# Thirteen float64 weight pieces loaded into buffers of their own at the start of a fused attention and MoE kernel

## The chip, the cores and the metric

One core of a Trainium2 chip runs the whole program in one launch. The metric is the device time of that core in microseconds (us), lower is better. Engines are named as the profile names them: PE is TensorE (PEld its weight loads), DVE is VectorE, ACT is ScalarE, POOL is GpSimd, SP is SyncE. A letter q behind a name (SPq, ACTq) marks the engine's own instruction queue, from which it also issues DMAs.

## The reference, cut to what matters

Windowed attention with sink tokens over 4 batches, 8 heads, 768 positions and head size 64, then a dense two-layer block with a squared ReLU, then a top-1 mixture of eight experts. The weights of the dense block come in as float64.

```
keep   = is_sink | (0 <= rel < window)
a      = softmax(where(keep, q @ k.T / 8, -1e9))
x      = (a @ v)  as [3072, 512]
h      = maximum(x @ moe_w_in, 0)            # moe_w_in  [512, 2048], float64
x      = (h * h) @ moe_w_out                 # moe_w_out [2048, 512], float64
e      = argmax(x @ w_gate)
out    = softmax(x @ w_gate)[e] * sigmoid(x @ w_output_gate[:, e]) * (maximum(x @ w1[e], 0) @ w2[e])
```

## The kernel before

The 3072 tokens go through attention and the dense block in NBLK = 12 blocks of 256 tokens, t = 0 to 11; after that comes the expert part in slots of 128 tokens. Matrices of the dense block are kept as a high and a low half in the PE's fast 4-byte type (float32r in the code), and a product is three matmuls (high by high, high by low, low by high). For the first two blocks (t below T32 = 2) attention uses plain float32 matmuls.

The float64 weights are brought in as 32 pieces, c = 0 to 31, by `conv(c)` (lines 261 to 285). Piece c = 2j is the j-th strip of moe_w_in (`WI[:, j]`), piece c = 2j + 1 the j-th strip of moe_w_out (`WO`, in two tiles WOa and WOb of eight strips each). A piece is one DMA of 512 KB on SP (L265 or L269) into a tile `craw` of 4 KB a partition, tag "stage", three buffers that set-up tiles and others share. Then its `rest()` runs: two ACT operations on the raw words (L275, L276), two DVE operations that join them to a float32 in `fbuf` (L278, L279), one copy that makes the high half, on ACT if c is a multiple of 3 and else on DVE (L281 or L283), and one POOL subtraction that makes the low half (L284). `fbuf` holds two pieces.

`cstep(n)` (lines 750 to 758) emits the loads two pieces ahead and then the `rest()` of the next n pieces. Thirteen calls stand between the attention steps of the first block (line 791, every third value of h from -39), before `split_x(0)` on line 793. In block t = 0, line 932 emits pieces 13 to 16 ahead of j = 0 and then one piece a step. The first layer of block t and step j, `l1(t, j)` (L546), reads strip 2j; the second layer, `l2` (L562), reads piece 2j + 1 two steps later.

Attention of a block is a list of events (`attn_events`) run at half steps: `prep_k` and `prep_q` transpose the loaded keys and queries (L319, L345), `scores` (L400, or L404 from t = 2 on), masks, exponentials and scaling on DVE and ACT (L408 to L424), `ptrans` (L439, L443), `pv` (L472, or L479 from t = 2 on). Attention of block t + 1 runs beside the dense layers of block t. The loads of keys, queries and values come from `loads(t, p)` two head pairs ahead, each into two buffers (L306). `split_x(t)` (L512, L513) makes both halves of a finished block's `xT`, which has one buffer: it marks the border between two blocks.

The order of instructions on each engine is fixed when the program is built: a planner takes instructions by priority when its cost model says that their inputs are there. Priority is program order, but attention events ahead of h = 0 are moved up by 200 and the dense layers of block 0 by 20 (lines 777 and 933); pieces and `split_x` are not moved. [...]

Of the kernel before, what the change touches and what calls it, by code (L numbers as in the profile page):

```python
# [8 lines left out]
F32 = mybir.dt.float32  # L9
F32R = mybir.dt.float32r  # L10
# [24 lines left out]
LEADS = ((5, 2, 4.5, 8.5), (5, 2, 4.5, 8), (5.5, 2.5, 4.5, 8))  # L35

SPLITS = {6: (0, 0), 8: (2, 0), 11: (0, 1), 12: (1, 0), 13: (2, 1), 14: (3, 0)}
NSLOT = NT // 128 + NE - 1
PRE = 2

# [2 lines left out]
def kern(ctx, tc, q, k, v, n_sink, window, w_in, w_out, w_gate, w_og, w1, w2, out):  # L43
# [216 lines left out]

    def conv(c):
        j, which = divmod(c, 2)
        raw = cv.tile([128, 512, 2], I32, tag="stage", bufs=3, name="craw")
        if which == 0:
            SY.dma_start(out=raw[:].rearrange("p (k f) w -> p k (f w)", k=4),  # L265
                         in_=w_in.bitcast(I32)[:, 256 * j:256 * j + 256].rearrange("(k p) f -> p k f", p=128))
            hi, lo = (WI[:, j, n].rearrange("p k f -> p (k f)") for n in range(2))
        else:
            SY.dma_start(out=raw[:].rearrange("p f w -> p (f w)"), in_=w_out.bitcast(I32)[128 * j:128 * j + 128, :])  # L269
            hi, lo = (WO[j // 8][:, j % 8, n] for n in range(2))  # L270

        def rest():
            L, Hh = raw[:, :, 0], raw[:, :, 1]

            A.activation(out=Hh.bitcast(F32), in_=Hh.bitcast(F32), func=AF.Copy, scale=2.0 ** -112)  # L275
            A.activation(out=L, in_=L.bitcast(U32), func=AF.Copy, scale=0.93 * 2.0 ** -29)  # L276
            f, fi = fbuf[:, c % 2], fbuf[:, c % 2].bitcast(I32)
            V.scalar_tensor_tensor(out=fi, in0=Hh, scalar=3, in1=L, op0=ALU.logical_shift_left, op1=ALU.bitwise_or)  # L278
            V.scalar_tensor_tensor(out=fi, in0=Hh, scalar=-2147483648, in1=fi, op0=ALU.bitwise_and, op1=ALU.bitwise_or)  # L279
            if c % 3 == 0:  # L280
                A.activation(out=hi, in_=f, func=AF.Copy)  # L281
            else:
                V.tensor_copy(out=hi, in_=f)  # L283
            G.tensor_tensor(out=lo, in0=f, in1=hi.bitcast(F32), op=ALU.subtract)  # L284
        return rest
# [9 lines left out]
    def loads(t, p):  # L295
        b, u = divmod(t, NQ // 2)
        s0 = 256 * u
        for nm, src, m in (("k", k, 3), ("q", q, 2), ("v", v, 3)):
            x = att.tile([128, m, 2, D], F32, tag=nm + "n", name=nm + "n", bufs=2)
            lo = s0 - 128 * (m - 2)  # L300
            o = 0
            if lo < 0:
                lo, o = 0, 1
            nb = m - o
            for e in range(2):
                (A if nm == "q" and t == 0 and p < 2 else SY).dma_start(out=x[:, o:m, e, :],  # L306
                             in_=src[b, 2 * p + e, lo:lo + 128 * nb, :].rearrange("(n s) d -> s n d", s=128))
            nat[nm, t, p] = x
# [438 lines left out]
    rests = {}  # L747
    st_ = dict(load=0, done=0)

    def cstep(n):  # L750
        for _ in range(n):
            if st_["done"] >= NC:
                return
            while st_["load"] < min(NC, st_["done"] + 2):
                rests[st_["load"]] = conv(st_["load"])
                st_["load"] += 1
            rests.pop(st_["done"])()
            st_["done"] += 1

# [5 lines left out]
    with tc.If(gv > 0):  # L765
        with tc.tile_pool(name="genp", bufs=1) as gp_:
            general(gp_)
    wpool2 = ctx.enter_context(tc.tile_pool(name="wpool2", bufs=1))
    WO[1] = wpool2.tile([128, NF // 2, 2, 512], F32R, name="WOb")
    WOf[1] = WO[1][:].rearrange("p j a f -> p (j a f)")  # L770
    events = sorted((e for t in range(NBLK) for e in attn_events(t)), key=lambda e: e[0])
    events.reverse()

# [13 lines left out]
    for h in range(-46, 0):  # L787
# [2 lines left out]
            setup2()  # L790
        if h >= -39 and h % 3 == 0:
            cstep(1)
    split_x(0)

    raw = None
# [303 lines left out]
```

## Time and profile before

| | us |
|---|---|
| median of 3 runs | 1198.46 (1195.75 to 1199.82) |
| the profiled execution | 1196.3 |
| its span in the trace | 1194.5 |
| start to `split_x(0)` | about 59 |
| block t = 0, to `split_x(1)` | 59 to 155.4 |
| a later block | some 60 to 62 |

The span is what the trace covers; 1.8 us of the profiled execution lie around it. Busy times are sums over an engine's instructions within a stretch; a matmul's end is modelled, so a busy PE can still run below its full pace. A table by stretch shows first the length, then each engine's busy time with the number of instructions, then the granted clock of TensorE as a share of full speed, the DMA engines' busy share and their rate.

### The profile page before, as it was taken

The numbers are of one execution on the slowest core, as the hardware profiler recorded it, in microseconds if no ns is written. First come the engines' busy times: TensorE is split into PE (matmuls) and PEld (weight loads), VectorE is DVE, ScalarE is ACT, GpSimd is POOL, SyncE is SP. The second block draws the span as 40 slices with busy tenths as digits, with TensorE's granted clock in tenths as the row PEclk, the third lists the DMA queues.
The fourth block names the chain that finished last, engine by engine and source line by source line (L and its number), as shares of the span: only waits on it lengthen the run. The fifth ranks groups of instructions, "written<-read, shape, count | busy, mean of one in ns | idle before, by whom it ended". The sixth has DMA issues, their size and how long they took to land. (4 is left out here: it accounts for less than half of the span.)

```text
span 1194.5 us, 24037 instructions
## 1 busy us (share of the span) xinstructions
PE 1138.7 (95%) x7022; PEld 945.7 (79%) x7022; DVE 761.5 (64%) x2123; ACT 626.5 (52%) x1740; POOL 457.9 (38%) x949
## 2 busy tenths in 40 slices
PE   4898889999999999999999999999899999999996
PEld 2476678888888888888888888887788888888884
DVE  4699776767676667676767677656611466764153
ACT  3677576767666766666676666545222222222200
POOL 4256665326565335555424556310211222222111
PEclk9999899999999999999999999999999999999998
DMA  4565411111211211121112120087411357554110
GB/s 123 132 181 176 137 35 45 32 51 37 54 32 28 50 37 46 35 49 29 47 35 51 37 54 1 19 182 207 133 39 44 100 179 255 189 203 151 42 51 23
DMA packets 139387, 100.08 MB, mean 84 GB/s; under 512 B 103903, under 2 KB 112223, under 8 KB 139234
## 3 DMA queue, kind: packets, MB, share of 16 engines
q1 hardware_dynamic: 132674, 83.85, 25.1%
q0 software_dynamic: 5472, 14.19, 3.6%
q8 instruction: 64, 1.05, 0.4%
q14 instruction: 89, 0.73, 0.3%
q10 hardware_dynamic: 1088, 0.26, 0.1%
HBM read 85.56 MB, written 13.76 MB: 83 GB/s over the span
## 5 line engine op out<-in xcount | busy, mean ns | idle before, releaser
L546 PE MATMUL psh<-xT,WI 128*128 128x256 f32 x2304 | 314.8, 285 | 10.6 <-POOL WI L284 8.1
L546 PEld LDWEIGHTS psh<-xT,WI 128*128 128x128 f32 x2304 | 294.9, 190 | 29.0 <-POOL WI L284 10.9
L867 PE MATMUL psh<-WI,xt 128*128 (+1 forms) x672 | 164.8, 400 | 0.3 <-ACT ht L847 0.3
L562 PE MATMUL psx<-WOb,h 128*128 128x512 f32 x576 | 157.8, 410 | 2.7 <-ACT h L552 2.4
L562 PE MATMUL psx<-WOa,h 128*128 128x512 f32 x576 | 159.0, 409 | 0.0
L867 PEld LDWEIGHTS psh<-WI,xt 128*128 128x128 f32 x672 | 124.3, 188 | 27.9 <-ACT xt L847 0.5
L550 DVE TENSOR_TENSOR r<-r 128x256 f32<-128x256 f32 x184 | 83.6, 455 | 68.3 <-ACT r L549 66.7
L562 PEld LDWEIGHTS psx<-WOb,h 128*128 128x128 f32 x576 | 102.6, 191 | 23.4 <-ACT h L552 3.9
L412 ACT ACTIVATE P<-P,st 128x260 f32<-128x260 f32 (+1 forms) x192 | 92.7, 485 | 47.4 <-DVE st L410 45.1
L883 DVE TENSOR_TENSOR ht<-psht,ht 128x512 fp32r<-128x512 f32 x56 | 38.5, 689 | 123.9 <-ACT ht L847 123.5
L549 ACT ACTIVATE r<-psh 128x256 f32<-128x256 f32 x192 | 72.2, 377 | 83.6 <-PE psh L546 72.4
L562 PEld LDWEIGHTS psx<-WOa,h 128*128 128x128 f32 x576 | 102.1, 190 | 17.4 <-issue 0.3
L553 DVE TENSOR_TENSOR h<-r,h 128x256 fp32r<-128x256 f32 x192 | 91.9, 479 | 29.3 <-ACT h L552 25.7
L905 POOL DMA_INDIRECT out_dram<-xg,pidx x28 | 31.2, 1116 | 193.5 <-ACT xg L904 152.0
L408 DVE CUSTOM_DVE_ANT_0 P<-pss,M 128x260 f32<-128x260 f32 (+1 forms) x184 | 72.5, 403 | 28.2 <-PE pss L404 14.3
L455 POOL TENSOR_SCALAR_AFFINE_SELECT PT<-PT 128x256 fp32r<-128x256 f32 x224 | 85.1, 415 | 12.9 <-DVE st L410 12.8
L552 ACT ACTIVATE h<-r 128x256 fp32r<-128x256 f32 x192 | 78.1, 408 | 22.2 <-DVE r L550 18.0
L896 PE MATMUL psy<-WOb,ht 128*128 (+1 forms) x336 | 85.1, 402 | 0.0
L896 PE MATMUL psy<-WOa,ht 128*128 (+1 forms) x336 | 84.1, 397 | 0.0
L873 ACT ACTIVATE r<-psh 128x512 f32<-128x512 f32 x48 | 28.7, 598 | 99.7 <-PE psh L867 97.8
L838 POOL DMA_INDIRECT xg<-x2tab,pidx x30 | 40.7, 1356 | 95.5 <-issue 55.9
L489 POOL TENSOR_TENSOR xr<-tB,tC 128x128 f32<-128x128 f32 x80 | 37.6, 470 | 97.8 <-DVE tB L488 95.3
(430 smaller groups left out, 1979.3 us busy)
## 6 DMA issues: line engine op xcount, KB each, us to landing
raw<-in_moe_w_dram SPq DMA_DIRECT2D x36, 1024.0 KB, 6.2
craw<-in_moe_w_in_dram SPq DMA_DIRECT2D x16, 512.0 KB, 3.8
craw<-in_moe_w_out_dram SPq DMA_DIRECT2D x16, 512.0 KB, 3.2
x2tab<-x2s SPq DMA_DIRECT2D x24, 256.5 KB, 3.1
kn<-in_k_dram SPq DMA_DIRECT2D x64, 96.0 KB, 2.3
vn<-in_v_dram SPq DMA_DIRECT2D x64, 96.0 KB, 2.2
qn<-in_q_dram SPq DMA_DIRECT2D x92, 64.0 KB, 2.1
kn<-in_k_dram SPq DMA_DIRECT2D x32, 64.0 KB, 2.1
```

Of the source, the lines that this page charges most:

```text
L408: V.tensor_tensor_reduce(out=P[:, e, 0:W], in0=ps[e][:, 0:W], in1=mask[:, 0:W], scale=1.0, scalar=-3.0e38, op0=ALU.add, op1=ALU.max, accum ...
L412: A.activation(out=P[:, e, 0:W], in_=P[:, e, 0:W], func=AF.Exp, scale=SCALE, bias=st[:, 2 + e:3 + e], accum_out=st[:, 4 + e:5 + e])
L455: G.affine_select(out=both[:, 1 - b, e], in_=bf[:, 0, e], pattern=[[0, 2], [1 - 2 * b, 128]], compare_op=ALU.is_gt if b else ALU.is_ge, fi ...
L546: PE.matmul(ps[:], lhsT=WI[:, j, a_, kk, :], rhs=x[:, b_, kk, :], start=(n == 0), stop=(n == 11))
L549: A.activation(out=hq[:], in_=ps[:], func=AF.Relu)
L550: (G if t == 0 and j % 2 else V).tensor_tensor(out=hq[:], in0=hq[:], in1=hq[:], op=ALU.mult)
L552: A.activation(out=o[:, 0], in_=hq[:], func=AF.Copy)
L553: V.tensor_tensor(out=o[:, 1], in0=hq[:], in1=o[:, 0].bitcast(F32), op=ALU.subtract)
L562: PE.matmul(acc[t][m][:], lhsT=o[:, a_, 128 * m:128 * m + 128], rhs=WO[j // 8][:, j % 8, b_, :], start=(j == 0 and n == 0), stop=(j == NF ...
L838: G.indirect_dma_start(out=x, out_offset=None, in_=x2tab[:] if s >= PRE else x2tab[0:256 * (NBLK - 3)], in_offset=bass.IndirectOffsetOnAxi ...
L867: PE.matmul(ps[:], lhsT=o[:, a_, kk, :], rhs=wview(n, par + 2048 * b_ + 512 * kk, 512), start=(c == 0), stop=(c == 11))
L896: PE.matmul(yp[s][:], lhsT=o[:, a_, kk, :], rhs=wview(2 + n, par + 2048 * b_ + 512 * kk, 512), start=(n == 0 and kk == 0 and c == 0), stop ...
```

## The change

The first thirteen pieces get buffers of their own: six raw tiles `braw` and four float32 tiles in `bf`, in a pool "boot" that takes the place of WOb until the prologue is over (WOb is allocated after it is closed). The first six loads are issued at once on ACT's queue, right after the branch of the general case; loads 6 to 12 stay on SP, each into the raw tile of the piece six before it. From piece 13 on the stage tiles, `fbuf` and the distance of two pieces are as before. The high half is made on ACT unless c mod 3 is 1, so ten pieces (c = 2, 5, ... 29) go from DVE to ACT. The tiles of loaded values get a third buffer.

```diff
+NBOOT, BRAW = 13, 6
...
     def conv(c):
         j, which = divmod(c, 2)
-        raw = cv.tile([128, 512, 2], I32, tag="stage", bufs=3, name="craw")
+        if c < NBOOT:
+            raw = braw[c % BRAW]
+        else:
+            raw = cv.tile([128, 512, 2], I32, tag="stage", bufs=3, name="craw")
+        eng = A if c < BRAW else SY
         if which == 0:
-            SY.dma_start(out=raw[:].rearrange("p (k f) w -> p k (f w)", k=4),
+            eng.dma_start(out=raw[:].rearrange("p (k f) w -> p k (f w)", k=4),
...
-            f, fi = fbuf[:, c % 2], fbuf[:, c % 2].bitcast(I32)
+            f = bf[:, c % 4] if c < NBOOT else fbuf[:, c % 2]
+            fi = f.bitcast(I32)
...
-            if c % 3 == 0:
+            if c % 3 != 1:
                 A.activation(out=hi, in_=f, func=AF.Copy)
             else:
                 V.tensor_copy(out=hi, in_=f)
...
-            x = att.tile([128, m, 2, D], F32, tag=nm + "n", name=nm + "n", bufs=2)
+            x = att.tile([128, m, 2, D], F32, tag=nm + "n", name=nm + "n", bufs=3 if nm == "v" else 2)
...
+    def fetch():
+        while st_["load"] < max(min(NBOOT, st_["done"] + BRAW), min(NC, st_["done"] + 2)):
+            rests[st_["load"]] = conv(st_["load"])
+            st_["load"] += 1
+
     def cstep(n):
         for _ in range(n):
             if st_["done"] >= NC:
                 return
-            while st_["load"] < min(NC, st_["done"] + 2):
-                rests[st_["load"]] = conv(st_["load"])
-                st_["load"] += 1
+            fetch()
             rests.pop(st_["done"])()
             st_["done"] += 1
...
-    wpool2 = ctx.enter_context(tc.tile_pool(name="wpool2", bufs=1))
-    WO[1] = wpool2.tile([128, NF // 2, 2, 512], F32R, name="WOb")
-    WOf[1] = WO[1][:].rearrange("p j a f -> p (j a f)")
+    bootS = ExitStack()
+    boot = bootS.enter_context(tc.tile_pool(name="boot", bufs=1))
+    braw = [boot.tile([128, 512, 2], I32, name=f"braw{n}") for n in range(BRAW)]
+    bf = boot.tile([128, 4, 512], F32, name="bf")
+    fetch()
...
             cstep(1)
+    bootS.close()
+    wpool2 = ctx.enter_context(tc.tile_pool(name="wpool2", bufs=1))
+    WO[1] = wpool2.tile([128, NF // 2, 2, 512], F32R, name="WOb")
+    WOf[1] = WO[1][:].rearrange("p j a f -> p (j a f)")
     split_x(0)
```

## Rows read from the trace of the kernel before

**Rows 1.** The page's first part: busy time of an engine, its share of the span, and its instructions.

```profile
PE 1138.7 (95%) x7022; PEld 945.7 (79%) x7022; DVE 761.5 (64%) x2123; ACT 626.5 (52%) x1740; POOL 457.9 (38%) x949
```

**Rows 2.** Busy time by stretch: the prologue, block 0, block 1, and a later block. Columns: stretch, its length, busy time and instructions of PE, PEld, DVE, ACT and POOL, granted clock, DMA share, GB/s.

```profile
12.00:59.00 47.00, 37.94 (x138) 20.69 (x138) 28.14 (x106) 28.23 (x83) 13.59 (x35) 1.00 0.45 121
59.00:155.40 96.40, 84.05 (x442) 60.69 (x440) 88.51 (x178) 63.55 (x153) 61.47 (x77) 0.93 0.55 160
155.40:215.00 59.60, 58.94 (x428) 51.44 (x429) 42.17 (x151) 42.33 (x134) 32.69 (x85) 1.00 0.15 36
...
340.00:402.20 62.20, 60.76 (x441) 52.94 (x441) 43.98 (x156) 41.78 (x132) 32.39 (x83) 1.00 0.14 35
```

**Rows 3.** PE's waits in block 0 (59 to 155.4 us): who waited for whom, us in total, times, longest.

```profile
PE psh L546 <- POOL WI L284: 8.1, 8, 2.3
PE psh L546 <- DVE WI L283: 2.3, 3, 1.7
```

**Rows 4.** Busy time by stretch again, a stretch of 5 us within block 0; the granted clock stands third from the end.

```profile
135.00:140.00 5.00, 5.00 (x14) 3.22 (x14) 1.24 (x5) 1.51 (x4) 2.43 (x5) 0.50 0.47 149
```

**Rows 5.** Instructions in order of time near the end of block 0 (start, duration, engine, line): the low half of the last strip of moe_w_in on POOL, and the first-layer matmuls that read it.

```profile
149.92 1.71 POOL L284 TENSOR_TENSOR WI<-fbuf,WI 128x512 fp32r<-128x512 f32 x1
...
151.67 1.44 PE L546 MATMUL psh<-xT,WI 128*128 128x256 f32 x10 [1.22 <-POOL WI L284]
```

**Rows 6.** DVE's groups of instructions in block 0 (61.8 to 155.5 us): line, names, shapes, count, busy us, mean ns, idle before.

```profile
L278 DVE SCALAR_TENSOR_TENSOR fbuf<-craw 128x512 int32<-128x512 int32 x25 | 23.7, 948 | 4.2 <-ACT craw L276 3.4 <-POOL V L364 0.7 <-POOL psk L427 0.2
L279 DVE SCALAR_TENSOR_TENSOR fbuf<-craw,fbuf 128x512 int32<-128x512 int32 x25 | 20.4, 818 | 0.0
...
L414 DVE TENSOR_SCALAR st<-st 128x2 f32<-128x2 f32 x8 | 5.0, 621 | 0.0
...
L283 DVE CAST WOb<-fbuf 128x512 fp32r<-128x512 f32 x6 | 2.5, 417 | 0.0
```

**Rows 7.** DVE's groups in the prologue (12 to 59 us), same columns.

```profile
L279 DVE SCALAR_TENSOR_TENSOR fbuf<-craw,fbuf 128x512 int32<-128x512 int32 x6 | 4.1, 689 | 0.0
L278 DVE SCALAR_TENSOR_TENSOR fbuf<-craw 128x512 int32<-128x512 int32 x6 | 4.1, 684 | 3.9 <-ACT craw L276 3.9
...
L414 DVE TENSOR_SCALAR st<-st 128x2 f32<-128x2 f32 x10 | 1.6, 160 | 0.3 <-ACT P L412 0.3
```

**Rows 8.** PE's groups that differ between block 0 (61.8 to 155.5 us, the first two lines) and a later block (340 to 402.3 us, the last two lines), same columns.

```profile
L472 PE MATMUL pso<-PT,vn 128*64 128x128 f32 x56 | 9.5, 312 | 0.0
L439 PE MATMUL pspt<-ident,P 128*128 128x128 f32 x30 | 7.1, 306 | 0.1
...
L479 PE MATMUL pso<-PT,V 128*128 128x256 f32 x32 | 5.1, 281 | 0.0
...
L439 PE MATMUL pspt<-ident,P 128*128 128x128 f32 x16 | 3.5, 301 | 0.0
```

**Rows 9.** SP's DMA issues in order of time in the prologue: start, duration of the issue, line, what is loaded.

```profile
20.92 0.44 SPq L269 DMA_DIRECT2D craw<-in_moe_w_out_dram  x1
28.39 0.88 SPq L306 DMA_DIRECT2D vn<-in_v_dram  x2
...
32.47 0.42 SPq L265 DMA_DIRECT2D craw<-in_moe_w_in_dram  x1
...
43.09 0.40 SPq L269 DMA_DIRECT2D craw<-in_moe_w_out_dram  x1
```

**Rows 10.** Waits of SP's queue and of ACT in the prologue (12 to 62 us and 12 to 59 us): who waited for whom, us in total, times, longest.

```profile
SPq L306 <- PE psh L472: 19.7, 5, 7.1
...
ACT craw L275 <- SPq L765: 8.7, 1, 8.7
```

**Rows 11.** DMA issues of the whole span: what is loaded, queue, count, KB each, median us from issue to landing.

```profile
craw<-in_moe_w_in_dram SPq DMA_DIRECT2D x16, 512.0 KB, 3.8
```

**Rows 12.** PE in order of time in the prologue: the last product with the values (L472) of each of the four head pairs of block 0, by which a pair's attention ends.

```profile
27.24 1.12 PE L472 MATMUL psh<-PT,vn 128*64 128x128 f32 x4
...
35.13 1.13 PE L472 MATMUL psh<-PT,vn 128*64 128x128 f32 x8
...
44.45 1.13 PE L472 MATMUL psh<-PT,vn 128*64 128x128 f32 x8
...
56.03 0.69 PE L472 MATMUL psh<-PT,vn 128*64 128x128 f32 x2
```

**Rows 13.** DVE in order of time in the prologue: the first joining operation (L278) of five of the pieces.

```profile
18.03 0.68 DVE L278 SCALAR_TENSOR_TENSOR fbuf<-craw 128x512 int32<-128x512 int32 x1
...
35.64 0.68 DVE L278 SCALAR_TENSOR_TENSOR fbuf<-craw 128x512 int32<-128x512 int32 x1
...
41.51 0.69 DVE L278 SCALAR_TENSOR_TENSOR fbuf<-craw 128x512 int32<-128x512 int32 x1
...
45.66 0.68 DVE L278 SCALAR_TENSOR_TENSOR fbuf<-craw 128x512 int32<-128x512 int32 x1
...
53.11 0.69 DVE L278 SCALAR_TENSOR_TENSOR fbuf<-craw 128x512 int32<-128x512 int32 x1
```

**Rows 14.** The load of the keys of head pair 2 of block 0 on SP, and the first transpose of these keys on PE, in order of time.

```profile
14.40 0.89 SPq L306 DMA_DIRECT2D kn<-in_k_dram  x2
...
25.81 0.48 PE L319 MATMUL psk__758<-ident,kn 128*128 128x128 f32 x1
```

More of the change, by code (lines that the diff above doesn't have):

```diff
@@ L268, in conv @@
         else:
-            SY.dma_start(out=raw[:].rearrange("p f w -> p (f w)"), in_=w_out.bitcast(I32)[128 * j:128 * j + 128, :])
+            eng.dma_start(out=raw[:].rearrange("p f w -> p (f w)"), in_=w_out.bitcast(I32)[128 * j:128 * j + 128, :])
             hi, lo = (WO[j // 8][:, j % 8, n] for n in range(2))
```

## The prediction

> **What bounds the kernel now.** I read the page's busy shares first, then busy time by stretch, then the waits and groups inside the stretch that stands out. Over the whole span PE is busy 95% and DVE 64% [rows 1], which looks like a kernel bound by matmuls with nothing left on the vector side. The table by stretch says otherwise for its head [rows 2]. A later block takes 62.2 us with PE busy for 60.8 of them. Block 0 runs about the same number of matmuls (442 against 441 records) in 96.4 us; there DVE is busy for 88.5 us, twice the 44 us of a later block, while PE's granted clock averages 0.93. So block 0 runs at the pace of DVE, and what DVE has there that later blocks don't have is the conversion of the float64 pieces.
>
> The waits agree: in block 0 PE stands 8.1 + 2.3 = 10.4 us for the halves of moe_w_in [rows 3]. After such a stall the clock goes too: 0.50, the lower of its two levels, throughout 135 to 140 us [rows 4]. And the block's last strip is just in time: its low half is ready at 149.92 + 1.71 = 151.6 us, and the matmuls that read it start at 151.67 [rows 5]. When the last pieces are done sets when block 0 ends.
>
> The prologue is the other half of the picture: from 12 to 59 us DVE is busy for 28.1 us of 47, ACT for 28.2 [rows 2]. Only six of the pieces are joined there [rows 7], so 26 of 32 fall into the block where DVE has no room. Why so few? The loads came late. After 20.92 us SP issues no piece until 32.47, and the next after that at 43.09 [rows 9]: its queue stands at a load of values, whose buffer is free only after a product with the values (19.7 us in five waits, 7.1 the longest) [rows 10]. A piece takes 3.8 us to land [rows 11], so it is the order of the queue that holds the pieces back. DVE's joins show the hole: none starts between 18.03 and 35.64 us [rows 13].
>
> **The change, part by part.**
>
> *Loads.* Six loads leave SP's queue and go out on ACT's, ahead of everything that the values can block. Each issue takes about 0.44 us of the issuing engine [rows 9], 2.6 us in all. ACT stands idle for 8.7 us before its first piece operation [rows 10], so this is hidden; without that cover it would cost 2.6 us. SP's order gets six issues shorter, and the third buffer for values takes away most of the 19.7 us of waiting. What SP then waits for is a raw tile six pieces back; behind such a wait stand the loads of keys and queries. These have slack: the keys of pair 2 were issued at 14.40 and used at 25.81 us [rows 14]. Six loads at once are 3.1 MB. At the 512 KB in 3.8 us of a single load [rows 11] they would need 23 us in a row and end near 31 us; overlapping can only make it less. So all six are there before the time at which the third piece was joined (35.64) [rows 13]. No direct cost.
>
> [...]
>
> *Pieces that move.* With loads no longer late, thirteen pieces can be converted ahead of `split_x(0)` where six were: seven leave block 0. One piece costs DVE there 0.948 + 0.818 us for the joins and, for two in three, 0.417 us for the high half [rows 6], that is 2.04 us. Its subtraction on POOL also slows DVE: the 2-element L414 takes 0.621 us on average in block 0 and 0.160 in the prologue [rows 6, 7], 8 x 0.46 = 3.7 us over 26 pieces, 0.14 each. Seven pieces: 7 x 2.18 = 15.3 us of DVE time.
>
> [...]
>
> *High halves on ACT.* Ten pieces go from DVE to ACT; of pieces 13 to 31, six (14, 17, ... 29). DVE loses 6 x 0.417 = 2.5 us in block 0 [rows 6]. ACT is busy for 63.6 of 96.4 us there [rows 2] and takes them in its idle time.
>
> *Block 0, summed.* DVE's 88.5 us become 88.5 - 15.3 - 2.5 = 70.7. What is late next is PE. An estimate of its need: a later block's 62.2 us, plus the products with values, 9.5 against 5.1, and the transposes, 7.1 against 3.5 [rows 8], so 70.2 us. The two engines are now even. I keep the 7.9 us by which block 0 was longer than DVE's work (96.4 - 88.5): 78.6 us, a gain of 17.8. Ends: at best PE's need alone, 70.2, a gain of 26.2; at worst only three of the seven pieces move, 3 x 2.18 + 2.5 = 9.0.
>
> *The prologue pays.* Seven more pieces run between the steps of a chain in which attention of block 0 goes from engine to engine; an instruction of a piece that an engine has just begun holds up the next link. The trace shows what that does: the four pairs end at 28.4, 36.3, 45.6 and 56.7 us [rows 12], so pair 1 took 7.9 us with no join ahead of its end but the one at 35.64, pair 2 took 9.3 with the join at 41.51 and the rest of the piece begun at 35.64, pair 3 took 11.1 with those at 45.66 and 53.11 [rows 13]. Pair 2 gives (9.3 - 7.9)/2 = 0.7 us for a piece; pair 3 gives 1.6, but attention of block 1 has begun beside it. Below there is nothing to gain, since the pairs' inputs were early [rows 14]; the lower end is 0. I take 0.7, the cleaner of the two: 7 x 0.7 = 4.9 us, ends 0 and 11.2.
>
> *After block 0.* Blocks from 1 on are filled by PE (58.9 of 59.6 us in block 1) [rows 2], and nothing of the change touches them. A gain at 155 us goes through to the end.
>
> *Sum.* -17.8 + 4.9 = -12.9 us. Against the profiled execution's 1196.3 that is 1183.4; the median of the runs lies 2.2 us above that execution, so 1198.5 - 12.9 = **1185.6 us**. With the ends of the prologue's cost the forecast's own range is 1181 to 1192.
>
> **The rivals.**
>
> *1. PE alone is the bound.* If DVE really gets free, the clock stays at its upper level too and block 0 falls to 70.2 us. With half of the prologue's cost: -26.2 + 2.4 = -23.8, 1174.7 us. For it: the clock's dip stands behind a stall for a piece. Against it: DVE needs 70.7 us itself, and both engines work in a fixed order.
>
> *2. The pieces only change place.* The prologue grows by what block 0 loses on them, 15.3 us, because there too each piece stops the chain. Only the six high halves are left: -2.5, 1196.0 us. For it: pair 3's 1.6 us. Against it: 18.9 us of idle DVE from 12 to 59 us.
>
> *3. The change doesn't do what it says.* The pieces are loaded early but the fixed order still runs them after `split_x(0)`, or SP's waits for raw tiles hold back pieces 6 to 12. Again -2.5, 1196.0 us. Against it: pieces stand ahead of `split_x` in program order, and in the trace only late loads let it pass them.
>
> *4. Slower.* The place is DVE's queue from 12 to 59 us. If the chain meets each added piece in full, both joins (0.68 + 0.69) and then a subtraction as long as the 1.71 us of [rows 5], the prologue grows by 7 x 3.08 = 21.6 us against a gain of 17.8 in the block: +3.8, 1202.3 us, and with the block's low end 9.0, 1211. It decides from a prologue longer by 21.4 us, that is an end of pair 3 near 78 us.
>
> **How the numbers follow.** Chances: the forecast 0.59, rival 1 0.13, rival 2 0.12, rival 3 0.07, rival 4 0.09. 0.3% is 3.6 us, about what a measurement of this kernel can tell from no change. The forecast and rival 1 are faster by more: 0.72. Rivals 2 and 3 lie within: 0.19. Rival 4 is slower: 0.09. The range runs from rival 1 to past rivals 2 and 3, 1174 to 1199 us, leaving out rival 4 and what lies beyond rival 1's estimate.
>
> **What would show it.** Six issues of pieces on ACT's queue in a row near 8 us; joins of pieces between 18 and 36 us; twelve or thirteen joins ahead of `split_x(0)`, and that near 64 us (forecast), 59 to 61 (rival 1), 74 (rival 2) or past 78 (rival 4). Block 0 near 79 us, DVE busy for about 71 of them, PE's waits for halves of moe_w_in well under 10.4 us and the clock above 0.93. Blocks 1 to 11 unchanged. The prediction is wrong if fewer than ten pieces are joined before `split_x(0)`, or if block 0 stays above 88 us although they were.

## The result, and the profile after

The changed kernel is slower: 1212.53 us median (1209.52 to 1213.36) against 1197.11 (1192.90 to 1199.82) on the same chip, ratio 1.0127 with a 95% interval of 1.0103 to 1.0150. The forecast was 1185.6, faster. The profiled execution took 1213.36 us, its span 1211.4 against 1194.5.

Lines of the changed kernel are shifted: loads L272 and L276, scalings L282 and L283, joins L286 and L287, high half L289 (ACT) or L291 (DVE), low half L292, `split_x` L520 and L521, first layer L554, its relu L557, second layer L570. The page's first part answers to [rows 1]; the engines' totals have hardly moved, so the time lies in the order, not in the work:

```profile
PE 1139.9 (94%) x7022; PEld 947.5 (78%) x7022; DVE 764.0 (63%) x2113; ACT 631.8 (52%) x1750; POOL 462.2 (38%) x949
```

Busy time by stretch, columns as in [rows 2]: the prologue, the part of it after attention, block 0, five microseconds of block 0, block 1.

```profile
12.00:79.80 67.80, 43.25 (x154) 23.15 (x154) 41.62 (x124) 38.36 (x101) 22.12 (x43) 1.00 0.57 164
61.50:79.80 18.30, 0.00 (x0) 0.00 (x0) 18.30 (x23) 11.32 (x20) 12.08 (x8) 1.00 0.44 142
79.80:174.20 94.40, 81.43 (x433) 61.70 (x434) 78.55 (x154) 60.10 (x148) 54.96 (x75) 0.93 0.40 116
...
155.00:160.00 5.00, 5.00 (x17) 3.43 (x16) 2.20 (x7) 1.47 (x5) 0.00 (x0) 0.50 0.13 28
174.20:233.00 58.80, 58.43 (x424) 50.80 (x423) 41.30 (x151) 41.59 (x133) 30.37 (x78) 1.00 0.15 38
```

The borders say where the time is. `split_x(0)` moved from 59 to 79.8 us (+20.8), `split_x(1)` from 155.4 to 174.2 (+18.8), the span's end by +16.9. Block 0, in which 21 joins are left of 26, is shorter by 2.0 us only, and its clock dips as before [rows 4]. The loss is the stretch from 61.5 to 79.8 us, in which PE does nothing. PE's waits in block 0 and the stretch ahead of it (59 to 174 us; answers to [rows 3]): the waits for halves are gone, and two for `xT` have come.

```profile
PE psh L554 <- ACT xT L520: 18.8, 1, 18.8
PE psh L554 <- ACT r L557: 4.9, 6, 2.5
PE psh L554 <- DVE xT L521: 4.3, 1, 4.3
```

Why `xT` is late is read from ACT's instructions in order of time (ACTq are its DMA issues):

```profile
13.59 0.38 ACTq L272 DMA_DIRECT2D braw<-in_moe_w_in_dram  x1
13.99 0.53 ACTq L276 DMA_DIRECT2D braw<-in_moe_w_out_dram  x1
14.55 0.60 ACTq L272 DMA_DIRECT2D braw<-in_moe_w_in_dram  x1
...
21.14 0.35 ACTq L276 DMA_DIRECT2D braw<-in_moe_w_out_dram  x1
21.53 0.28 ACT L482 ACTIVATE xr<-psh 128x128 f32<-128x128 f32 x1 [3.00 <-DMA braw<-in_moe_w_in_dram]
...
28.81 0.37 ACTq L272 DMA_DIRECT2D braw<-in_moe_w_in_dram  x1
...
36.90 0.35 ACTq L276 DMA_DIRECT2D braw<-in_moe_w_out_dram  x1
...
42.50 0.67 ACT L282 ACTIVATE braw<-braw 128x512 f32<-128x512 f32 x1
...
56.88 0.67 ACT L282 ACTIVATE braw<-braw 128x512 f32<-128x512 f32 x1
...
79.83 1.32 ACT L520 ACTIVATE xT<-xr 128x256 fp32r<-128x256 f32 x4
```

The six loads don't leave in a row near 8 us. They stand in ACT's stream between attention's exponentials and copies, over 23 us. The fourth also holds ACT up: the 3.00 us of idle time in the row behind it end when an earlier load has landed, by 21.1 us. And the scalings are later than the loads: the first piece is scaled at 42.50, 28.9 us after its load was issued, with no idle time of ACT just before it, because the fixed order has it there. DVE's joins follow; the first three (answer to [rows 13], where the first is at 18.03 or earlier):

```profile
48.03 0.69 DVE L286 SCALAR_TENSOR_TENSOR bf<-braw 128x512 int32<-128x512 int32 x1
...
54.39 0.69 DVE L286 SCALAR_TENSOR_TENSOR bf<-braw 128x512 int32<-128x512 int32 x1
...
58.36 0.69 DVE L286 SCALAR_TENSOR_TENSOR bf<-braw 128x512 int32<-128x512 int32 x1
```

Two joins lie ahead of 56 us. Attention itself got faster: pair 3 ends at 53.9 us, 2.8 earlier than in [rows 12]. Then everything that had come late runs in one bulk, the conversion of nine pieces from 56.9 to 79.8 us on ACT, DVE and POOL, all of it ahead of `split_x(0)`, which has no priority and stands behind them in program order. PE in order of time:

```profile
53.22 0.69 PE L480 MATMUL psh<-PT,vn 128*64 128x128 f32 x2
...
80.28 0.80 PE L554 MATMUL psh<-xT,WI 128*128 128x256 f32 x2 [18.81 <-ACT xT L520]
...
85.40 4.85 PE L554 MATMUL psh<-xT,WI 128*128 128x256 f32 x21 [4.32 <-DVE xT L521]
```

### The profile page after: what moved, and what is told of

Its sections match the earlier page's. It is cut to its first block, busy times and chain, and to the rows that moved or that the text cites. A ratio compares the mean times of both kernels' runs of the same rounds, so it can differ in the third digit from the quotient of the medians.

```text
span 1211.4 us, 24030 instructions
## 1 busy us (share of the span) xinstructions
PE 1139.9 (94%) x7022; PEld 947.5 (78%) x7022; DVE 764.0 (63%) x2113; ACT 631.8 (52%) x1750; POOL 462.2 (38%) x949
## 5 line engine op out<-in xcount | busy, mean ns | idle before, releaser
L554 PE MATMUL psh<-xT,WI 128*128 128x256 f32 x2304 | 316.7, 286 | 28.0 <-ACT xT L520 18.8
L554 PEld LDWEIGHTS psh<-xT,WI 128*128 128x128 f32 x2304 | 296.8, 191 | 44.8 <-ACT xT L520 19.5
L570 PE MATMUL psx<-WOa,h 128*128 128x512 f32 x576 | 157.8, 408 | 1.5 <-DVE h L561 1.5
L570 PE MATMUL psx<-WOb,h 128*128 128x512 f32 x576 | 156.2, 409 | 0.8 <-ACT h L560 0.4
L570 PEld LDWEIGHTS psx<-WOb,h 128*128 128x128 f32 x576 | 102.9, 191 | 21.2 <-ACT h L560 1.5
L570 PEld LDWEIGHTS psx<-WOa,h 128*128 128x128 f32 x576 | 101.2, 189 | 19.3 <-DVE h L561 2.0
L557 ACT ACTIVATE r<-psh 128x256 f32<-128x256 f32 x192 | 72.3, 377 | 74.0 <-PE psh L554 63.4
L416 DVE CUSTOM_DVE_ANT_0 P<-pss,M 128x260 f32<-128x260 f32 (+1 forms) x184 | 72.7, 403 | 31.3 <-PE pss L412 17.0
L463 POOL TENSOR_SCALAR_AFFINE_SELECT PT<-PT 128x256 fp32r<-128x256 f32 x224 | 84.4, 412 | 12.6 <-DVE st L418 12.5
L913 PE MATMUL psy<-WOb,ht 128*128 (+1 forms) x336 | 85.1, 402 | 0.0
L855 POOL DMA_INDIRECT xg<-x2tab,pidx x30 | 45.6, 1519 | 95.8 <-issue 54.4
```

Of the source, the lines that this page charges most:

```text
L416: V.tensor_tensor_reduce(out=P[:, e, 0:W], in0=ps[e][:, 0:W], in1=mask[:, 0:W], scale=1.0, scalar=-3.0e38, op0=ALU.add, op1=ALU.max, accum ...
L463: G.affine_select(out=both[:, 1 - b, e], in_=bf[:, 0, e], pattern=[[0, 2], [1 - 2 * b, 128]], compare_op=ALU.is_gt if b else ALU.is_ge, fi ...
L554: PE.matmul(ps[:], lhsT=WI[:, j, a_, kk, :], rhs=x[:, b_, kk, :], start=(n == 0), stop=(n == 11))
L557: A.activation(out=hq[:], in_=ps[:], func=AF.Relu)
L570: PE.matmul(acc[t][m][:], lhsT=o[:, a_, 128 * m:128 * m + 128], rhs=WO[j // 8][:, j % 8, b_, :], start=(j == 0 and n == 0), stop=(j == NF ...
L855: G.indirect_dma_start(out=x, out_offset=None, in_=x2tab[:] if s >= PRE else x2tab[0:256 * (NBLK - 3)], in_offset=bass.IndirectOffsetOnAxi ...
```

## The experiments

My first theory was the late loads and the bulk. Its rivals were the bulk's place alone, the small parts of the change, and then the forecast's own frame: that block 0 runs at DVE's pace, so that pieces taken out of it are worth 2.2 us each. All medians stand against the kernel before on the same chip (1193.6 to 1194.9). "Start" is the first instruction of `split_x(0)`, "joined" the pieces whose first join came before it, "block 0" the time from there to `split_x(1)`, all of the profiled execution; "idle" is block 0 without PE's busy time, "clock" its granted clock. The executions of one kernel differ by up to some 11 us (e5: 1209.89 to 1220.67; before: 1192.90 to 1199.82), and the profiled ones of e5 and e9 were their fastest, 7.8 and 4.2 us below the median, so small differences between rows from "start" on say little. Kernels without a median leave weights out, so that later routing differs; each of them was run once.

| kernel | median | ratio | start | joined | block 0 | idle | clock |
|---|---|---|---|---|---|---|---|
| before | 1197.11 | 1 | 59.0 | 6 | 96.4 | 12.4 | 0.93 |
| after | 1212.53 | 1.0127 (1.0103-1.0150) | 79.8 | 11 | 94.4 | 13.0 | 0.93 |
| e1 loads on SP | 1199.83 | 1.0038 (1.0019-1.0057) | 59.5 | 5 | 99.8 | 14.9 | 0.91 |
| e2 split_x first | 1211.98 | 1.0147 (1.0116-1.0179) | 54.1 | 2 | 120.8 | 28.1 | 0.93 |
| e11 block first | 1217.12 | 1.0185 (1.0142-1.0228) | 54.0 | 2 | 120.4 | 29.1 | 0.89 |
| e5 loads first | 1217.71 | 1.0203 (1.0177-1.0229) | 72.7 | 12 | 98.6 | 14.9 | 0.86 |
| e6 spread | 1205.01 | 1.0084 (1.0060-1.0108) | 70.7 | 8 | 95.3 | 14.9 | 0.93 |
| e8 all early | 1209.15 | 1.0114 (1.0086-1.0141) | 81.0 | 16 | 89.7 | 5.0 | 0.92 |
| e3 high halves | 1201.22 | 1.0053 (1.0034-1.0072) | 51.8 | 5 | 104.9 | 18.2 | 0.89 |
| e4 third v | 1203.40 | 1.0069 (1.0043-1.0095) | 58.2 | 6 | 101.9 | 12.5 | 0.90 |
| e7 buffers only | 1206.36 | 1.0103 (1.0080-1.0125) | 56.0 | 6 | 110.3 | 21.9 | 0.89 |
| e9 more joins | 1209.79 | 1.0124 (1.0081-1.0168) | 56.8 | 6 | 103.8 | 17.4 | 0.89 |
| e10 fewer joins | | | 59.0 | 6 | 96.7 | 11.1 | 0.91 |
| e13 no piece in block 0 | | | 64.0 | 6 | 76.7 | 1.3 | 1.00 |
| e14 no pieces | | | 65.7 | 0 | 74.2 | 0.1 | 0.97 |
| e15 without 6 to 12 | | | 57.8 | 6 | 97.2 | 10.0 | 0.91 |
| e16 without last 7 | | | 60.6 | 6 | 86.6 | 8.4 | 1.00 |
| e12 priority 40 | 1197.05 | 1.0016 (0.9996-1.0035) | 56.7 | 6 | 95.4 | 14.7 | 0.95 |
| e17 before, earlier | 1200.63 | 1.0050 (1.0033-1.0067) | 59.0 | 6 | 98.1 | 16.7 | 0.97 |
| e18 mended | 1203.13 | 1.0073 (1.0046-1.0099) | 57.5 | 5 | 103.0 | 22.9 | 0.93 |

**e1: all loads on SP.**

```diff
-        eng = A if c < BRAW else SY
+        eng = SY
```

> The changed kernel with all thirteen early loads on SP's queue again; buffers, high halves and third value buffer stay. Theory (queue): the six loads on ACT's queue stand behind the first block's attention, so no piece is joined before 48 us, and then all thirteen run ahead of split_x(0), which leaves PE idle for 18.8 us. With SP as the issuer joins start near 14 us again, at most seven pieces stand ahead of split_x(0), which comes at 58 to 62 us, and PE's wait of 18.8 us is gone: 1192 to 1199 us. Rival (load of work): ACT's extra high halves and the pieces' own buffers, not the queue, fill the engines; then split_x(0) stays past 75 us and the time at 1208 to 1214.

The change cost 15.4 us against the kernel before on its chip, e1 costs 4.9: some 10.5 us come back (the two intervals leave some 4 us either way), and the empty stretch with them, so the engine that issues the loads is the largest part of the loss. It isn't that the loads come sooner on SP. Each of the six leaves later than in the changed kernel, the last at 48.78 instead of 36.90 us, and yet the first join is at 20.76 instead of 48.03:

```profile
13.92 0.38 SPq L272 DMA_DIRECT2D braw<-in_moe_w_in_dram  x1
...
48.78 0.48 SPq L276 DMA_DIRECT2D braw<-in_moe_w_out_dram  x1
```

```profile
20.76 0.69 DVE L286 SCALAR_TENSOR_TENSOR bf<-braw 128x512 int32<-128x512 int32 x1
```

What changed with the issuing engine is the place of the conversions in the fixed order: four of them between attention's steps instead of one bulk behind it. Why the planner puts them there, no run shows. What is left of the loss is hardly in the prologue (59.5), mostly in block 0 (99.8).

**e2 and e11: the bulk's place.** The loads stay on ACT; e2 moves `split_x(0)` up, e11 the dense layers of block 0 as well.

```diff
-    split_x(0)
+    with tc.high_priority(400):
+        split_x(0)
...
-        with (tc.high_priority(20) if t == 0 else ExitStack()):   # e11 only
+        with (tc.high_priority(400) if t == 0 else ExitStack()):
```

> The changed kernel with split_x(0) moved up in priority by 400, the loads left on ACT's queue. Theory (queue and priority): split_x(0) comes near 61 us, PE's wait of 18.8 us before the first layer goes; but the eleven pieces that ran in that gap now fall into block 0, so that 30 of 32 are joined there at some 3.3 us each, about 100 us: block 0 ends near 162 us instead of 174, and the time is 1199 to 1205 us. Rival (order doesn't matter, the sum of DVE's work up to the last piece does): block 0 still ends near 174 us and the time stays 1210 to 1214.

> The changed kernel with split_x(0) and the dense layers of block 0 raised to priority 400, so that the bulk of pieces stands behind them wherever their inputs allow. Theory (the 15 us come from the order bulk against block 0): the wait of PE for the first relu and for split_x(0), 25.7 and 18.8 us in the two kernels so far, falls under 8 us, and the time to 1199 to 1205 us. Rival (the loads on ScalarE's queue are late whatever the order; PE then waits for strips instead): the waits for WI grow by the same 15 us, 1208 to 1216 us.

In e2 the start comes at 54.1, and the bulk then stands in front of the first relu. PE's longest wait there was 20.9 us:

```profile
PE psh L554 <- ACT r L557: 25.7, 6, 20.9
```

In e11 no wait is longer than 2 us, but there are many, 29.1 us of idle in all, and the clock drops to 0.89. PE waits there for halves of moe_w_in for 12.8 us, which the changed kernel doesn't; e2's rival named the time, e11's missed it by 1.1 us. So the bulk's place ahead of `split_x(0)` isn't what costs the time: with 2 pieces joined at 54 us, where the kernel before has 6, block 0 takes some 24 us more in either order. How it pays differs. In e2, as in the changed kernel, the pieces catch up: 12 and 11 are joined by 80 us, 13 in the kernel before, and the last one starts its join at 148.70 and 148.72, against 149.50. What is lost is the time in which PE stands while they do, 20.9 and 18.8 us. In e11 they stay behind, with 8 joined by 80 us and the last at 171.40:

```profile
171.40 0.68 DVE L286 SCALAR_TENSOR_TENSOR fbuf<-craw 128x512 int32<-128x512 int32 x1
```

**e5, e6, e8: pieces really early.** Do we get the forecast once thirteen pieces are joined in time? e5 raises the first six loads (still on ACT); e6 and e8 issue them on SP and raise the pieces of the prologue too.

```diff
-    fetch()
+    with tc.high_priority(400):
+        fetch()
...
-            cstep(1)
+            with tc.high_priority(60):      # e6; 200 in e8; not in e5
+                cstep(1)
```

> The changed kernel with its six loads on ACT's queue moved up in priority by 400, so that they really go out at once, ahead of attention. Theory (late issue): after issued them at 13.6, 14.0, 14.6, 21.1, 28.8 and 36.9 us, between attention's instructions, and no piece was joined before 48 us. Now all six are issued within 3 us of the first, joins start before 22 us, some four pieces are done among attention's steps, and the stretch without PE ahead of the first layer falls from 18.8 us to 8 to 14: 1200 to 1208 us. Rival (the pieces' low priority, not the loads, keeps them after attention): joins still start past 40 us, the wait stays at 17 to 20 us, 1209 to 1214.

> The changed kernel with all early loads on SP, the first six moved up by 400 and the thirteen pieces moved up by 60, so that they are spread over the prologue: eleven pieces are begun ahead of split_x(0). This is what the forecast had supposed. Forecast's theory: split_x(0) comes at 62 to 68 us, block 0 takes 78 to 84 us with DVE busy for some 71, 1184 to 1192 us. Rival (block 0 doesn't follow the number of its pieces: after took 94.4 us for it with 21 joins): block 0 still takes over 90 us, 1198 to 1206 us.

> As the spread kernel, with the pieces moved up by 200, as far as attention itself: all thirteen are begun ahead of split_x(0). Forecast's theory with 0.7 us of prologue for a piece: split_x(0) at 64 to 70 us, block 0 at 75 to 82 us, 1182 to 1192 us. Rival (in the prologue a piece at attention's priority stops the chain in full, 3 us each): split_x(0) past 76 us, 1198 to 1210 us.

In e5 twelve pieces are joined ahead of `split_x(0)`, which is what the forecast asked for, and the kernel is 2.0% slower, outside both ranges: the prologue is 13.7 us longer, and block 0 takes 98.6 us with 20 pieces in it. Little of this is pieces within attention's chain: attention ends at 56.5 us, no later than before, with five joined, and the other seven again stand in front of `split_x(0)`. What e5 adds is ACT waiting as an issuer. Its last three issues leave at 19.05, 21.30 and 22.89 us, with no other work of ACT between them; the idle time ahead of its first exponential ends when an earlier load has landed, and that exponential starts at 23.29 us, 8.1 later than in the changed kernel (15.20):

```profile
23.29 0.40 ACT L420 ACTIVATE P<-P,st 128x128 f32<-128x128 f32 x1 [19.91 <-DMA braw<-in_moe_w_out_dram]
```

In e8 the pieces do run within the chain, and attention ends at 80.6 us: ten more pieces make the prologue 22.0 us longer, 2.2 us each. In e6 it is 11.7 us longer with only two more joined (four more begun), so the price isn't one number. In both the rivals were right, in time and mark. PE's waits of e8 (12 to 82 us) show how: attention's chain is held by pieces on ACT and, in a wait that was 4.3 us in the kernel before too, on DVE. How much of it is the high halves, which are on ACT in e5, e6 and e8, wasn't tested.

```profile
PE pspt L447 <- ACT P L432: 16.6, 3, 10.4
PE pss L408 <- DVE bf L287: 5.2, 1, 5.2
```

And block 0, with ten pieces fewer than before, gains 6.7 us of it, 0.67 each. That left the question what block 0 runs at.

**e9, e10: is DVE its bound?** e9 writes the second join twice for pieces 13 to 31 (with no effect on the value), e10 leaves it out.

```diff
             V.scalar_tensor_tensor(out=fi, in0=Hh, scalar=-2147483648, in1=fi, op0=ALU.bitwise_and, op1=ALU.bitwise_or)
+            if c >= 13:      # e9: the same once more; e10 puts the one above under "if c < 13"
+                V.scalar_tensor_tensor(out=fi, in0=Hh, scalar=-2147483648, in1=fi, op0=ALU.bitwise_and, op1=ALU.bitwise_or)
```

> The kernel before with the second join written out twice for pieces 13 to 31 (the second time it changes nothing): 19 x 0.82 = 15.5 us more DVE work in block 0, no other work added. Theory of the prediction (block 0 runs at DVE's pace): block 0 grows by some 15 us, from 96.4 to 110 to 113 us, the whole to 1208 to 1212. Rival (block 0 is held by PE's own need and by single waits, DVE has slack): it grows by 0.25 to 0.35 of that, 4 to 6 us, the whole 1198 to 1202.

> The kernel before without the second join (the sign bit) for pieces 13 to 31: 15.5 us less DVE work in block 0. It leaves out the signs of those weights, so later routing differs; only block 0 is read. Theory of the prediction: block 0 shrinks by some 15 us to 80 to 82 us, split_x(1) near 140. Rival: DVE wasn't the bound; block 0 shrinks by 2 to 6 us, split_x(1) at 149 to 153.

Block 0 of e10, by the table of stretches:

```profile
59.00:155.70 96.70, 85.63 (x450) 63.20 (x448) 76.01 (x161) 63.90 (x157) 55.89 (x79) 0.91 0.53 157
```

DVE has 12.5 us less to do than in [rows 2], and block 0 takes 96.7 us against 96.4. In this run the amount of DVE's work is not its bound; e15 below says the same with seven pieces left out. e9 adds 11.1 us of DVE time (99.59) and block 0 grows by 7.4, so DVE has no room to spare either:

```profile
56.80:160.60 103.80, 86.44 (x445) 62.80 (x444) 99.59 (x196) 63.87 (x154) 63.22 (x75) 0.89 0.51 148
```

(Its median, up by 15.0, is what the forecast's theory asked for; of the 9.2 us in the profiled span 5.2 lie ahead of `split_x(1)` and 4.0 behind it. The profiled execution was the fastest of four, so e9 by itself doesn't decide.) The forecast's theory asked for 80 to 82 and for 110 to 113; its rival for 90 to 94 and 100 to 102. e10 is outside both: nothing at all was gained.

**e13 to e16: what are the pieces worth?** Pieces are replaced by constants that POOL writes, and their loads are left out; only which ones differs.

```diff
+        light = c >= 6       # e13; e14: c >= 0; e15: 6 <= c < 13; e16: c >= 25
...
+            if light:
+                G.memset(hi.bitcast(F32), 2.0 ** -6)
+                G.memset(lo.bitcast(F32), 0.0)
+                return
```

> The kernel before with pieces 6 to 31 replaced by constants that GpSimd writes (two short writes for each), without their loads, scalings, joins and copies; it leaves out those weights, so later routing differs and only the prologue and block 0 are read. 26 pieces leave block 0. Theory of the prediction (2.18 us a piece until PE's need of 70.2 us): block 0 takes 70 to 72 us. Rival (fixed order and PE's real need, about 77 us at full clock by the busy time and the granted clock of block 0, with attention's own links on top): 80 to 88 us, so that all 26 pieces together are worth 9 to 16 us, some 0.5 us each.

> As the run before it, with pieces 0 to 5 replaced too, so that no piece is left anywhere; it leaves out all weights of the dense block. Theory of the prediction (0.7 us for a piece in the prologue): split_x(0) comes 3 to 5 us earlier than with six pieces. Rival (2 to 3 us for a piece): 12 to 18 us earlier, near 42 to 46 us.

> The kernel before with pieces 6 to 12, the seven that the change moves, replaced by constants that GpSimd writes (two writes of 0.52 us each, which may lengthen the prologue); it leaves out those weights, so later routing differs and only block 0's length is read. Theory of the prediction: 7 x 2.18 = 15.3 us less, block 0 near 81 us. Rival (the share that falls on seven of 26 pieces worth 20 us): 5 us less, near 91 us. Second rival (the last strips, not the first, set the end): no change, 95 to 97 us.

> The same with pieces 25 to 31 replaced in place of 6 to 12; it leaves out those weights. Theory of the prediction: 15.3 us less, 81 us, as it doesn't matter which. Rival (even share): 91 us. Second rival (the last strips set the end): 85 to 90 us, clearly less than without pieces 6 to 12, and PE's waits for halves after 125 us gone.

Block 0 of e13, e15 and e16, one answer each:

```profile
64.00:140.70 76.70, 75.39 (x458) 58.15 (x459) 35.36 (x122) 33.32 (x102) 21.63 (x60) 1.00 0.17 39
```

```profile
57.80:155.00 97.20, 87.16 (x458) 65.30 (x459) 74.31 (x173) 57.62 (x146) 56.36 (x79) 0.91 0.45 128
```

```profile
60.60:147.20 86.60, 78.18 (x442) 57.47 (x441) 73.76 (x159) 55.58 (x141) 48.36 (x74) 1.00 0.47 134
```

e13 is the floor: PE is busy for 75.4 of 76.7 us, at 1.00 in its row, so all 26 pieces together cost block 0 19.7 us, 0.76 each. (That is between its theory's 70 to 72 and its rival's 80 to 88; its block 0 begins 5 us later than in the kernel before.) e15 and e16 have the same number of pieces left in block 0 (19) and nearly the same DVE time (74.3, 73.8), and differ by 10.6 us. Without the seven pieces that the change moves, nothing is gained, which is e15's second rival; PE then waits for a relu instead of halves, and the half clock after the longest of these waits (2.67 us, ending at 131.62) holds to 145.3:

```profile
131.62 0.71 PE L551 MATMUL psh<-xT,WI 128*128 128x256 f32 x2 [2.67 <-ACT r L554]
```

```profile
135.00:140.00 5.00, 5.00 (x17) 3.57 (x17) 1.47 (x5) 0.70 (x2) 0.00 (x0) 0.50 0.00 0
140.00:145.00 5.00, 5.00 (x19) 3.22 (x18) 1.64 (x8) 1.28 (x6) 1.86 (x6) 0.50 0.31 71
```

Without the last seven the waits stay under 1.4 us and the clock at 1.00, as e16's second rival had it. e14 didn't answer its question (what a piece costs the prologue): beside the constant writes two instructions of DVE lasted 3.03 and 5.74 us (last section), and `split_x(0)` came at 65.7.

**e3, e4, e7: the parts alone.** e3 and e4 change the kernel before, e7 is the changed kernel with loads on SP and without these two.

```diff
-            if c % 3 == 0:                  # e3
+            if c % 3 != 1:
...
-            x = att.tile([128, m, 2, D], F32, tag=nm + "n", name=nm + "n", bufs=2)      # e4
+            x = att.tile([128, m, 2, D], F32, tag=nm + "n", name=nm + "n", bufs=3 if nm == "v" else 2)
```

> The kernel before with one part of the change alone: ten more high halves on ACT. Theory: DVE loses about 2.5 us of work in block 0 and ACT takes it in idle time: 0 to 4 us faster, 1193 to 1198. Rival (these halves are part of the loss): ACT's copies, 0.62 us each, hold up the chain of attention or of the first layer, 2 to 6 us slower.

> The kernel before with one part alone: the third buffer for values. Theory: SP's 19.7 us of waiting for products with the values shrinks and pieces are loaded earlier, but the two-piece distance of the loads still limits them to about seven pieces ahead of split_x(0): within 3 us of before, 1194 to 1200. Rival (earlier loads alone are harmful, since ready pieces go ahead of split_x(0)): split_x(0) comes over 5 us later and the time is over 1200.

> The buffers of the change alone: six raw tiles and four joined tiles for thirteen pieces, loads on SP; high halves as before, two value buffers. Theory (the loss beyond ACT's queue comes from the third value buffer and the high halves, +0.7% and +0.5% alone): as before, within 3 us, 1192 to 1198. Rival (the buffers themselves cost, because pieces 13 to 15 are loaded ahead of 6 to 12 and ready pieces crowd): 1199 to 1205.

Each loses by itself, 0.5 to 1.0%, where each theory had none or a gain, and together (e1, 0.4%) they lose no more than the least of them. In all three block 0 is longer, at a clock of 0.89 or 0.90 and, but for e4, with more idle time of PE.

**e12, e17, e18: order alone.** e12 moves block 0's layers up by 40 in place of 20, in the kernel before; e17 and e18 ask for the pieces of block 0 faster, in the kernel before and in e1.

```diff
-            cstep(max(2 * j + 3, 17 + j) - st_["done"])
+            cstep(max(2 * j + 3, 17 + j + j // 2) - st_["done"])
```

> The kernel before with the dense layers of block 0 moved up by 40 in place of 20: the same instructions in a slightly other order, nothing else. Theory (before sits in an order that any small reordering makes worse, which alone explains losses of 0.4 to 1%): +3 to +10 us, 1197 to 1204. Rival (small reorderings are neutral, so the buffers themselves cost): within 3 us of the kernel before.

> The kernel before with the pieces of block 0 asked for faster: three for every two steps in place of one a step (17 + j + j/2 in place of 17 + j), so that the last one is done by step 10 and not 15. Theory (PE's waits for the last strips and the clock behind them make 10 us of block 0): block 0 takes 88 to 92 us and the time falls by 4 to 8 us. Rival (the order only puts the stall at another place, where pieces then stand ahead of the dense layers): block 0 95 to 100 us, no change or slower by up to 5 us.

> The changed kernel with all loads on SyncE and the pieces of block 0 asked for faster, as in the run before it. Theory: block 0 falls from 99 to 100 us to 88 to 94 and the time to 1187 to 1193 us. Rival: as with the loads alone on SyncE, 1198 to 1203 us.

e12 makes no difference that can be told, so not every reordering loses. e17 loses 0.5%, as its rival had it, by 1.7 us more: what e16 gained by leaving the last pieces out can't be had by asking for them earlier. e18 is no better than e1. No version that I ran beats the kernel before.

## Why the prediction was wrong

**Loads: the step that failed first.** The forecast had the issues "hidden" in 8.7 us of ACT's idle time, at "No direct cost". I priced the issues, and they are cheap. What I didn't price is where they stand: the issues (0.35 to 0.60 us each) stand in ACT's own order, and attention's instructions, moved up by 200, took the places ahead of the last three; one of these then held ACT up for 3.00 us. The 8.7 us of idle time [rows 10] couldn't hide them: they end at 12.09 us, and the first issue left at 13.59. Above all the conversions moved in the fixed order, to behind attention. e1 measures issuing on ACT against SP at 10.5 us, all of these together. The mark of 8 us failed by the buffers and not by the queue: in every kernel with the new raw tiles the first load leaves at 11.7 to 14.3 us, on either engine, and in every one with the old at 7.5 to 8.4; what it waits for there is open. With the loads on SP and moved up the forecast would have failed all the same (e6 1.0084, e8 1.0114), by the next two steps.

**Pieces that move: 11 joined, of 12 or 13, but nine of them in a bulk.** My marks were `split_x(0)` near 64, or past 78 for rival 4. It came at 79.8, by another mechanism than rival 4's: no chain met the pieces one by one, attention ended early, and the pieces then stood in front of everything that PE needed. That the number joined came near the forecast's is luck.

**The prologue pays: mis-sized by a factor of three.** 0.7 us a piece was the difference of two pairs' lengths in the kernel before; where pieces really run within the chain they cost 2.2 us each (e8), in e6 5.9 for each of two more joined. The upper end, 1.6, was too low as well. Rival 4's 3.08 was nearer than 0.7.

**Block 0: the frame that failed.** Its 78.6 us came from "block 0 runs at the pace of DVE". It took 94.4, and the test that I set, wrong if it stays above 88, decides against me. e10 and e15 show that DVE's amount of work doesn't set its length: with 12.5 and 14.2 us of it taken away, block 0 takes 96.7 and 97.2. So a piece that leaves block 0 is not worth 2.18 us but 0.67 (e8) to 0.76 (e13), and nothing where it is one of the first (e15). With 2.2 us to pay for it in the prologue, the move gained nothing in any order that I ran.

What sets the length is PE: its need, its idle time in single waits, and the time that it loses at the half clock. With 76.7 us as need, the idle time of the table, and the lost share of the recorded clock (before and after, it leaves out a slower pace at the head of the block, last section), the sum gives 76.7 + 12.4 + 6.7 = 95.8 for the kernel before (96.4 measured), 96.3 after (94.4), 96.5 for e10 (96.7), 105.5 for e9 (103.8), 85.1 for e16 (86.6), 119.0 for e11 (120.4). Busy and idle add up by definition; what the sum shows is that the busy time, corrected for the clock, is nearly the same in these. It isn't in all: the sum gives 113.3 for e2 (120.8) and 105.4 for e5 (98.6), and why is open, but for the clock's record in e2 (last section). My estimate of PE's need, 70.2, was 6.5 us too low. And the reading that the last strip is just in time held for the end of the block (e16: 9.8 us), but I moved pieces of its beginning (e15: nothing).

**High halves, third buffer:** forecast as a gain of 2.5 us and as a help for SP. Alone they lose 0.5 and 0.7%. DVE's relief gave nothing, which agrees with e10; why they lose is open.

**After block 0: right.** From `split_x(1)` to the end of the span it is 1039.0 us before and 1037.2 after.

Open are the 4.9 us left in e1: they lie in block 0, in waits that differ from order to order, and no run isolates them. That the planner's order is what makes single waits of 2 us come and go is argued from e3, e4, e7 and e12, not shown.

## What to carry to other kernels

An engine that is busy for 92% of a stretch need not bound it: before pricing work that leaves it, take some of it away or double it, and see whether the stretch moves. Moved work has two prices, one where it leaves and one where it goes; measure both (here 0.67 to 0.76 against 2.2 us a piece). Work that came early but had a low place in the fixed order ended up in one lump in front of the next thing (nine pieces, from 56.9 to 79.8 us); ask of each moved DMA and each moved step not only whether its engine is idle, but which instructions will stand ahead of it and behind it. Where PE has many waits, look at each for what the clock does behind it.

## What the runs showed of the hardware

**In e14 two instructions of DVE lasted as long as a run of writes on POOL.** DVE and POOL in order of time:

```profile
41.96 3.03 DVE L415 TENSOR_SCALAR st<-st 128x2 f32<-128x2 f32 x1
45.02 0.17 DVE L420 RECIPROCAL st<-st 128x2 f32<-128x2 f32 x1
45.22 5.74 DVE L427 TENSOR_SCALAR P<-P,st 128x260 f32<-128x260 f32 x1
```

```profile
45.15 0.52 POOL L276 MEMSET WI<- 128x512 f32 x1
45.61 0.53 POOL L275 MEMSET WOb<- 128x512 f32 x1
...
49.81 0.52 POOL L276 MEMSET WOb<- 128x512 f32 x1
50.28 0.52 POOL L275 MEMSET WI<- 128x512 f32 x1
```

The two-element L415 takes 3.03 us here, and 0.17 us at 52.66 in the same run; L427 takes 5.74. Through both, POOL's writes of 0.52 us follow each other without a gap: L415 ends at 44.99 us, with a write that ends at 44.96, and L427 at 50.96, with the last of twelve writes in a row ending at 50.80. By what the one holds up the other, no run shows.

The same is seen, more mildly, beside single instructions of POOL. In the kernel before, L414 takes 0.15 to 0.18 us in 14 of 18 cases from 12 to 160 us; the three that start within a subtraction of POOL (L284) at 96.75, 106.79 and 130.16 us take 1.23, 1.28 and 1.23, and end 0.02 to 0.03 us behind it. In the changed kernel, a first join (L286) that starts at 74.31 us, within a subtraction (73.87 to 75.52), takes 1.76 us; the one at 78.08, with POOL idle, takes 0.68. The thirteen first joins take 1.18 us there on average, in e1 0.77.

```profile
L286 DVE SCALAR_TENSOR_TENSOR bf<-braw 128x512 int32<-128x512 int32 x13 | 15.2, 1180 | 0.0
```

So "busy" of DVE counts such time in full: 3.03 us for an instruction that takes 0.17 elsewhere. That this is why taking work away from it gave nothing is argued, not shown.

**The half clock outlived the wait.** After a wait of 2.5 us in the changed kernel, and after one of 2.67 us in e15, the clock stood at 0.50 for 13.5 us; before and after have no level in their traces but 0.50 and 1.00. My estimate of the cost, from the 13.5 us and the 0.50, is up to some 6.7 us, more than twice the wait itself. It wasn't always so long: after e15's wait of 2.50 us, which ended at 111.14, it was over after 3.5. Changed kernel first, then e15 twice:

```profile
152.30:165.80 13.50, 13.50 (x49) 9.48 (x48) 4.95 (x17) 3.71 (x12) 4.45 (x11) 0.50 0.18 40
```

```profile
111.30:114.60 3.30, 3.30 (x16) 3.30 (x17) 2.87 (x6) 2.90 (x6) 0.87 (x4) 0.50 0.09 29
131.80:145.30 13.50, 13.50 (x48) 9.00 (x49) 4.79 (x18) 2.94 (x10) 4.06 (x8) 0.50 0.13 29
```

**A row's 1.00 can hide the slower pace.** Behind the changed kernel's waits of 18.8 and 4.3 us for `xT` the rows say 1.00. But the same first-layer matmuls run 23 in 5.00 us (0.21 us from one to the next) until about 90.7 us, and then 21 in 2.20 (0.12). The slower pace is that of e15's row at 0.50 above (16 in 3.30). In e2, too, the eight matmuls that follow the 20.9 us take 1.85 us, in a row of 1.00 (80 to 90 us). It isn't these waits that brought the slower pace in the changed kernel: PE had it ahead of them. Its transposes (L447) take 0.42 us each (median) from 12 to 62 us and 0.27 from 90.9 to 152; in the kernel before (L439) 0.42 until 60 us and 0.27 from 81 to 131. The trace's clock record begins at 90.8 us after and at 63.5 before, and a row counts what lies ahead of that as 1.00. So in these two the table's clock leaves out the slower pace at the head of block 0.

```profile
85.40:90.40 5.00, 5.00 (x23) 5.00 (x24) 5.00 (x10) 3.31 (x6) 1.41 (x1) 1.00 0.02 3
90.90:93.10 2.20, 2.20 (x21) 2.20 (x21) 2.20 (x3) 1.81 (x6) 2.20 (x3) 1.00 0.91 254
```
